# The first block of a convolution and SiLU kernel: up matmuls on 128 rows without ordering reads, exponents clamped on GpSimd, splits on VectorE

## The chip, the cores and the metric

One Trainium2 chip; the kernel runs on one of its cores. The time is that of one execution on the device in microseconds, the median of several runs. The profile comes from one execution of its own.

## The reference

A lightweight convolution feeds a two-layer SiLU network, all in float32:

```
w   = softmax(weight)                    # 8 heads x 7 taps
y   = causal conv of x (8, 4096, 192) along the sequence, one filter for each group of 24 channels
h   = y.reshape(32768, 192) @ w_in       # w_in  192 x 2048, float64 in memory
out = (h * sigmoid(h)) @ w_out           # w_out 2048 x 192, float64 in memory
```

The two weight matrices arrive as 64-bit floats, and the kernel makes 32-bit floats of them with integer instructions on their two halves.

## The kernel before

The 32768 tokens are done in 32 blocks of 1024 (`TT`), each of two halves of 512 (`TB`). The 192 channels are three pieces of 64: pieces 0 and 1 stand on partitions 0 to 63 and 64 to 127 of one set of tiles (`nats[0]`, `xts[0]`, `xs[0]`), piece 2 of both halves on those of another (`nats[1]`, `xts[1]`, `xs[1]`). A value that goes into the up matmuls is split into a high part, a low part and a mixed one (`split` for x, `Unit` for the weights), in a type that TensorE takes in one pass.

`PLAN` is a written order of tokens that each block follows from the second on: loads, transposes, taps (`conv`), splits, up matmuls (`A`, `B` with `w_a`, `C`, `E` with `w_b`), a scaling of the sums in PSUM on ScalarE (`X`), SiLU (`S`), sums and down matmuls. Within a block a pair of up matmuls works on two halves of the array's rows, and the two write different banks. Before a bank is written from the other half of the rows, VectorE reads one column of it into `dot` (`T`, `U`): the next matmul on the bank waits for that read.

The first block goes its own way, as the weights must be made ready beside it. All instructions of an engine stay in the order in which the code issues them (`pin`), and each engine works through its own list; SP's list holds nearly all DMA issues. In order:

- x and w_in are asked for on SP and ACT. `load_in(j, part, queue)` brings a quarter `j` of w_in: part 0 is rows 0 to 127 (one DMA), part 1 rows 128 to 191 (two DMAs).
- The taps are made on TensorE from the softmax. Two sets of diagonal matrices (`diag_of`) let TensorE do the first block's convolution (`conv_on_pe`) in three pieces of 512 columns.
- Twelve `Unit`s convert the weights: for each quarter of w_in one of part 0 (512 words a partition, to `w_a`) and one of part 1 (256 words, to `w_b`), then four quarters of w_out (768 words, to `wd`). A unit takes the exponent bits (`exponent`), the sign of the low byte and the clamped exponent (`on_act`: a Sign and two Relus on ScalarE), the mantissa and a sticky bit, and puts the number together (`rounded`). A unit of w_in is then split: `high`, `scaled` on ScalarE, `lower`, `between` on VectorE, and for part 1 `spread` copies half of `w_b` to the other 64 partitions by two DMAs on the GpSimd queue. `work(u)` runs unit u together with the split of unit u - 1.
- `woven` interleaves those steps with the sixteen up tiles (`of_up`: quarter j, chunk c, two banks each) in the order of the code. In tile i's turn stand A and B of that tile and C, T, E, U, X, S of the one before.
- `load_out(q, queue)` asks for a quarter of w_out with two DMAs; the third and fourth reuse buffers that earlier units must have read.
- After the sixteenth tile come the down matmuls of the first block (`down_plain`, 96 on `g` and `wd`), the transposes, the stores, and on VectorE `combine_out`, which changes `wd` for the later blocks. The second block's loads, taps and splits (`first_`) run beside the down matmuls.

Nearly all instructions are issued through a wrapper, so the profile gives them line 142; matmuls of the blocks have line 457. They are told apart by their tiles: `g` (weights being converted, and SiLU's results), `ps` (the banks), `w_a`, `w_b`, `wd`, `xs`, `dot`.

Of the kernel before, what the change touches and what calls it, by code (L numbers as in the profile page):

```python
# [8 lines left out]
F32 = mybir.dt.float32  # L9
# [3 lines left out]
AF = mybir.ActivationFunctionType  # L13
ALU = mybir.AluOpType
# [4 lines left out]
def kernel(  # L19
# [17 lines left out]
    B, S, D = x.shape  # L37
    H, K = weight.shape
    NT = B * S
    DFF = moe_w_in.shape[1]  # L40
    P = 128
# [4 lines left out]
    TB = 512  # L46
# [3 lines left out]
    NJ = NCH // 4  # L50
    SQ = 32
    HT = TB // 2
    SPLIT = 4096.0
# [140 lines left out]
    def g_slot(j, c, n):  # L194
        return g_all[:, j // 2, 2 * c + n, j % 2, :]
# [25 lines left out]
    for sign, base in ((1, 0), (-1, grp - 1)):  # L221
# [18 lines left out]
        base=0,  # L240
# [25 lines left out]
    def load_in(j, part, queue):  # L266
        t = raw(("i", j))
        if part == 0:
            to = t[:, 0 : 2 * CA].rearrange("p (a e c) -> p a e c", a=2, e=2)
            queue.dma_start(out=to, in_=in_a[:, :, 2 * j : 2 * j + 2, :])  # L270
        else:
            to = t[:, 2 * CA : 2 * WC].rearrange("p (e c) -> p e c", e=2)
            for a in range(2):
                queue.dma_start(out=rows(to, a), in_=in_b[:, a, 2 * j : 2 * j + 2, :])

    def load_out(q, queue):
        t = raw(("o", q)).rearrange("p (a e d) -> p a e d", a=2, e=2)
        for a in range(2):
            queue.dma_start(out=t[:, a, :, :], in_=out32[a, q])
# [1 line left out]
    scratch = flat(g_all[:, 0, 8:11])  # L281
    low_all = flat(g_all[:, 1, 8])
    ONE = 1 << 20
    edges = const.tile([P, 2], F32, name="edges")
    vec.memset(edges[:, 0:1], float(1151 * ONE))
    vec.memset(edges[:, 1:2], float(255 * 8 * ONE))
    BELOW = 1.0 - 2.0**-13

    class Unit:
# [25 lines left out]

        def exponent(self):
            vec.tensor_single_scalar(self.ex, self.hi, 0x7FF * ONE, op=ALU.bitwise_and)

        def on_act(self):
            act.activation(self.st, self.byte, AF.Sign)  # L320
            act.activation(self.ex, self.ex, AF.Relu, bias=edges[:, 0:1], scale=-1.0)
            act.activation(self.ex, self.ex, AF.Relu, bias=edges[:, 1:2], scale=-8.0)

        def mantissa(self):
            vec.tensor_scalar(
# [17 lines left out]
                out=self.w, in0=m, scalar=2.0**-44, in1=self.ex.bitcast(F32), op0=ALU.mult, op1=ALU.mult  # L343
            )

        def high(self):
            act.activation(self.to[0], self.w, AF.Copy, scale=BELOW)

        def lower(self):
            vec.tensor_tensor(self.low, self.w, f32(self.to[0]), op=ALU.subtract)  # L350

        def scaled(self):
            act.activation(self.to[1], self.low, AF.Copy, scale=SPLIT)

# [23 lines left out]
    def heat(times):  # L378
        for _ in range(times):
# [35 lines left out]
    def turn_in(b, k):  # L415
        vec.transpose(xts[k][:, pad:], flat(nats[k]))
# [38 lines left out]

    def mm(to, lhs, rhs, start=False):
        return pin(nc.tensor.matmul(to, lhs, rhs, start=start, stop=True, skip_group_check=True))  # L457
# [140 lines left out]
    did.update((0, t) for t in base if t[0] in "QD" or t.split(".")[0] in (*SUMS, *PREP, "st"))  # L598

    units = [Unit(2 * j + part, ("i", j), part) for j in range(NJ) for part in range(2)]  # L600
    units += [Unit(q, ("o", q), None) for q in range(NJ)]

    def begin(u):
        if u < len(units):
            units[u].exponent()
            units[u].on_act()

    def work(u):

        now, was = (units[i] if 0 <= i < len(units) else None for i in (u, u - 1))  # L610
        split_ = was is not None and was.part is not None
        if split_:
            was.high()
        if now:
            now.mantissa()
        yield
        if split_:
            was.lower()
        if now:
            now.sticky()  # L620
        if split_:
            was.scaled()
        yield
        if split_:
            was.between()
            was.spread()
        yield
        if now:
            now.rounded()
            begin(u + 1)  # L630
            if now.key == ("o", 0):
                load_out(3, sync)
# [10 lines left out]
    diags = [flat(g_all[:, 0, s_])[:, 0 : K * P].rearrange("p (i c) -> p i c", c=P) for s_ in (6, 7)]  # L643

    def diag_of(k):
        for i in range(K):
            act.activation(diags[k][:, i, :], one_hot, AF.Copy, scale=taps[:, k, i : i + 1])

    def conv_on_pe(to, k, first):
        for i in range(K):  # L650
            mm(to, diags[k][:, i, :], xts[k][:, first + i : first + i + TB], start=i == 0)

    def drain(stream):
        for _ in stream:
            pass

    turn_in(0, 0)
    begin(0)
    diag_of(0)
    conv_on_pe(banks[0], 0, 0)  # L660
    turn_in(0, 1)
    halo_in(0, 2)
    drain(work(0))
    diag_of(1)
    conv_on_pe(banks[1], 0, TB)
    conv_on_pe(banks[2], 1, 0)
    split(0, 0, "h", banks[0], ts(0, TB))
    next_ = work(1)
    next(next_)
    split(0, 0, "l", banks[0], ts(0, TB))  # L670
    next(next_)
    split(0, 0, "d", banks[0], ts(0, TB))
    next(next_)
    drain(next_)
    split(0, 0, "h", banks[1], ts(1, TB))
    next_ = work(2)
    next(next_)
    split(0, 0, "l", banks[1], ts(1, TB))
    next(next_)
    split(0, 0, "d", banks[1], ts(1, TB))  # L680
    split(0, 1, "h", banks[2])
    next(next_)
    split(0, 1, "l", banks[2])
    split(0, 1, "d", banks[2])
    drain(next_)
    for _ in range(3):
        homes.append(homes.pop(0))

    def of_up(i):

        now = "%d%d" % divmod(i, 4) if i < 4 * NJ else ""
        was = "%d%d" % divmod(i - 1, 4) if i else ""
        for t in (["A.%s0", "C.%s", "T.%s"], ["B.%s0", "E.%s", "U.%s"], ["A.%s1", "X.%s0", "X.%s1"], ["B.%s1", "S.%s0", "S.%s1"]):
            who = now if t[0][0] == "A" else was
            if who:
                yield lambda t=t, who=who: [step(0, x_ % who) for x_ in t]

    def of_work(u):
        stream = work(u)
        for _ in range(4):  # L700
            yield lambda stream=stream: next(stream, None)
# [69 lines left out]
```

## Time and profile before

| what | us |
|---|---|
| median of 3 runs | 2286.57 (2285.32 to 2289.86) |
| profiled execution, its own time | 2284.52 |
| its span | 2282.8 |
| PE busy | 2238.4 (98%) |
| DVE busy | 1816.4 (80%) |
| ACT busy | 1323.4 (58%) |
| POOL busy | 14.8 (1%) |

PE is TensorE's matmuls, PEld its weight loads, DVE VectorE, ACT ScalarE, POOL GpSimd, SP the engine that issues DMAs. Times of rows count from the span's start. A row of an order in time reads: start, length, engine, line, operation, output <- input, shapes, count, and in brackets the idle time before it and what ended it. A row of waits reads: who waited for whom, us in total, times, longest. A row of groups reads: count | busy us, mean ns of one | idle time before and what ended it. Rows of one engine that follow each other can overlap a little, so one row's start to the next's is what an instruction takes in a full engine.

### The profile page before, as it was taken

Reading aid. Unit: us, or ns where it says so; the run is one execution under the profiler, and the core shown is the slowest. Engines: PE = TensorE matmul, PEld = TensorE weight load, DVE = VectorE, ACT = ScalarE, POOL = GpSimd, SP = SyncE. Lnnn points to the kernel's source line nnn. Section 1 sums busy time; section 2 is a strip of 40 time slices with the busy share of each in tenths; the row PEclk is TensorE's granted clock in tenths of the full one; section 3 lists DMA queues with packets and bytes.
Section 4 is the critical chain, followed back from the end, with each engine's and each line's share of the span. In section 5 each row is a group of like instructions: output and inputs, shape, how many; then the busy total and the mean of one; then the engine's idle time right before and its main releaser. Section 6 shows DMA issues by size and latency. Waiting matters only on the chain.

```text
span 2282.8 us, 47340 instructions
## 1 busy us (share of the span) xinstructions
PE 2238.4 (98%) x19386; PEld 1679.2 (74%) x19386; DVE 1816.4 (80%) x3049; ACT 1323.4 (58%) x2708; POOL 14.8 (1%) x58
## 2 busy tenths in 40 slices
PE   7789999999999999999999999999999999999998
PEld 4447777777777777777777777777777777777775
DVE  4658877888877888877888877888877888877866
ACT  5735666555666555666555566555566555566543
POOL 0000000000000000000000000000000000000000
PEclk8899999999999999999999999999999999999999
DMA  4210111011111011111011111011111011111001
GB/s 104 63 28 15 29 29 20 10 29 29 29 29 21 9 29 29 29 29 25 5 29 29 29 29 26 6 26 29 29 29 29 6 24 29 29 29 29 8 8 29
DMA packets 406122, 61.25 MB, mean 27 GB/s; under 512 B 401936, under 2 KB 403984, under 8 KB 405904
## 3 DMA queue, kind: packets, MB, share of 16 engines
q1 hardware_dynamic: 400176, 56.00, 14.4%
q8 instruction: 151, 2.47, 0.5%
q0 software_dynamic: 512, 1.57, 0.3%
q10 hardware_dynamic: 5216, 0.66, 0.2%
q14 instruction: 67, 0.55, 0.1%
HBM read 31.46 MB, written 25.17 MB: 25 GB/s over the span
## 4 chain that ended last, share of the span: by engine, by line
PE 97%; ACT 1%; DMA 1%; DVE 1%; SPq 0%; issue 0%; DVEq 0%; ACTq 0%
PE ps L457 97%; ACT g L142 1%; ACT ps L142 0%; DMA w_b<-w_b 0%; SPq L142 0%; DMA g<-in_moe_w_in_dram 0%; DVE g L142 0%; DVE wd L142 0%; DVE fin L142 0%; ACT w_b L142 0%; DVE xs L142 0%; ACT L142 0%; ACT wd L142 0%; DVE dot L142 0%; DVE w_a L142 0%
## 5 line engine op out<-in xcount | busy, mean ns | idle before, releaser
L457 PE MATMUL ps<-g,wd 128*64 128x256 f32 (+1 forms) x10112 | 1127.2, 384 | 0.0
L457 PEld LDWEIGHTS ps<-g,wd 128*64 128x64 f32 x10112 | 720.5, 137 | 396.9 <-issue 36.0
L142 DVE TENSOR_TENSOR g<-g 128x1024 f32<-128x1024 f32 x806 | 951.2, 1218 | 9.2 <-PE ps L457 5.6
L457 PE MATMUL ps<-xs,w_a 64*128 64x512 f32 x6144 | 899.6, 393 | 22.2 <-DVE dot L142 15.5
L142 ACT ACTIVATE ps<-ps 128x512 f32<-128x512 f32 (+1 forms) x1117 | 585.1, 581 | 313.7 <-PE ps L457 265.9
L457 PEld LDWEIGHTS ps<-xs,w_a 64*128 64x128 f32 x6144 | 639.2, 185 | 124.2 <-DVE dot L142 34.2
L142 ACT ACTIVATE g<-ps 128x512 f32<-128x512 f32 x1024 | 561.3, 616 | 50.2 <-PE ps L457 41.8
L457 PE MATMUL ps<-xs,w_b 64*128 64x512 f32 x3072 | 537.2, 394 | 7.2 <-DMA w_b<-w_b 7.2
L142 DVE COPY dot<-ps 128x1 f32<-128x1 f32 x1024 | 160.6, 157 | 382.1 <-PE ps L457 372.2
L457 PEld LDWEIGHTS ps<-xs,w_b 64*128 64x128 f32 x3072 | 330.5, 186 | 54.8 <-issue 11.5
L142 DVE SCALAR_TENSOR_TENSOR nat<-xt,taps,nat 128x1024 f32<-128x1024 f32 (+1 forms) x372 | 368.8, 1005 | 1.8 <-ACT nat L142 1.4
L142 ACT COPY fin<-ps 128x256 f32<-128x256 f32 (+1 forms) x127 | 47.8, 376 | 424.1 <-PE ps L457 424.1
L142 DVE TENSOR_TENSOR fin<-fin,ps 128x256 f32<-128x256 f32 x248 | 95.6, 404 | 19.2 <-PE ps L457 19.2
L142 DVE STREAM_TRANSPOSE fin<-fin 128x256 f32<-128x256 f32 (+1 forms) x189 | 83.0, 440 | 17.2 <-ACT fin L142 15.9
L142 ACT ACTIVATE nat<-xt,taps 128x1024 f32<-128x1024 f32 (+1 forms) x62 | 57.9, 936 | 16.3 <-DVE xt L142 14.5
L142 DVE STREAM_TRANSPOSE xt<-nat 128x512 f32<-128x512 f32 (+1 forms) x64 | 61.5, 963 | 3.5 <-ACT xt L142 2.5
L142 DVE SCALAR_TENSOR_TENSOR xs<-xs 128x512 fp32r<-128x512 f32 x65 | 60.9, 937 | 0.2
L142 DVE TENSOR_TENSOR xs<-nat,xs 128x1024 fp32r<-128x1024 f32 (+1 forms) x62 | 59.0, 952 | 0.0
L142 ACT ACTIVATE xs<-nat 128x1024 fp32r<-128x1024 f32 (+1 forms) x62 | 52.5, 846 | 10.9 <-DVE nat L142 10.9
L142 ACT ACTIVATE fin<-ps 128x256 f32<-128x256 f32 x93 | 35.8, 385 | 39.6 <-PE ps L457 39.6
L142 ACT COPY xt<-xt 64x6 f32<-64x6 f32 x56 | 10.9, 195 | 52.9 <-DVE xt L142 52.3
L142 ACT COPY ps<-zeros 128x256 f32<-128x256 f32 x62 | 23.6, 381 | 1.0
(58 smaller groups left out, 204.7 us busy)
## 6 DMA issues: line engine op xcount, KB each, us to landing
out_dram<-fin SPq DMA_DIRECT2D x244, 96.0 KB, 2.5
nat<-in_x_dram SPq DMA_DIRECT2D x126, 128.0 KB, 3.0
nat<-in_x_dram SPq DMA_DIRECT2D x128, 64.0 KB, 2.4
g<-in_moe_w_out_dram SPq DMA_DIRECT2D x4, 384.0 KB, 7.3
w_b<-w_b POOLq DMA_DIRECT2D x8, 192.0 KB, 3.0
fin<-in_moe_w_out_dram SPq DMA_DIRECT2D x4, 384.0 KB, 4.8
g<-in_moe_w_in_dram SPq DMA_DIRECT2D x2, 512.0 KB, 5.2
fin<-in_moe_w_in_dram SPq DMA_DIRECT2D x2, 512.0 KB, 6.8
```

Source lines behind the costliest of these rows:

```text
L142: return lambda *args, **kw: pin(getattr(self.engine, name)(*args, **kw))
L457: return pin(nc.tensor.matmul(to, lhs, rhs, start=start, stop=True, skip_group_check=True))
```

## The change

Only the first block's code changes, and the conversion of the weights.

- Up matmuls of the first block: `A` and `B` use all 128 rows, both pieces of channels in one matmul, one bank after the other; `C` and `E` keep 64 rows each, one bank each. `T` and `U` are gone. The order by tiles is A of tile i, then B, E and S of tile i - 2, then C and X of tile i; A of the first three tiles stands ahead of the loop.
- A unit's clamped exponent is made by two GpSimd instructions in place of ScalarE's two Relus; the Sign stays on ScalarE. `high` goes to VectorE, so a unit's split is three VectorE instructions and one of ScalarE, and it comes in the unit's own `work`. The next unit's exponent stands at the beginning of `work`.
- Part 1 of each quarter of w_in (with `spread`) is loaded and converted ahead of part 0, and `spread` is issued on SP's queue.
- The convolution of the third piece is done by ScalarE and VectorE (`conv(0, 1, i)`) in place of TensorE; the diagonal matrices are made once, and stand ahead of the first unit. A SiLU on one column, with its table load, stands behind the exponential of the softmax.

```diff
@@ Unit
         def exponent(self):
             vec.tensor_single_scalar(self.ex, self.hi, 0x7FF * ONE, op=ALU.bitwise_and)
-
-        def on_act(self):
             act.activation(self.st, self.byte, AF.Sign)
-            act.activation(self.ex, self.ex, AF.Relu, bias=edges[:, 0:1], scale=-1.0)
-            act.activation(self.ex, self.ex, AF.Relu, bias=edges[:, 1:2], scale=-8.0)
+            pool.tensor_scalar(
+                self.ex, self.ex, scalar1=float(896 * ONE), scalar2=float(1151 * ONE), op0=ALU.max, op1=ALU.min
+            )
+            pool.tensor_scalar(
+                self.ex, self.ex, scalar1=float(896 * ONE), scalar2=8.0, op0=ALU.subtract, op1=ALU.mult
+            )
...
-        def high(self):
-            act.activation(self.to[0], self.w, AF.Copy, scale=BELOW)
-
-        def lower(self):
+        def split(self):
+            vec.tensor_scalar(self.to[0], self.w, scalar1=BELOW, scalar2=None, op0=ALU.mult)
             vec.tensor_tensor(self.low, self.w, f32(self.to[0]), op=ALU.subtract)
-
-        def scaled(self):
             act.activation(self.to[1], self.low, AF.Copy, scale=SPLIT)
-
-        def between(self):
             vec.scalar_tensor_tensor(
...
         def spread(self):
             if self.part:
                 for a in range(2):
-                    pool.dma_start(
+                    sync.dma_start(
...
+    load_in(0, 1, sync)
     load_in(0, 0, sync)
...
+    act.activation(warm, warm, AF.Silu)
     for i in range(4, 8):
         load(0, i, sync)
-    load_in(0, 1, sync)
     for j in (1, 2, 3):
-        for part in range(2):
+        for part in (1, 0):
             load_in(j, part, sync)
...
-    units = [Unit(2 * j + part, ("i", j), part) for j in range(NJ) for part in range(2)]
+    units = [Unit(2 * j + i, ("i", j), 1 - i) for j in range(NJ) for i in range(2)]
...
+        now = units[u]
+        begin(u + 1)
+        now.mantissa()
+        now.sticky()
         yield
+        now.rounded()
+        if now.key == ("o", 0):
+            load_out(3, sync)
         yield
+        if now.part is not None:
+            now.split()
+            now.spread()
         yield
...
+    def up_first(what, i):
+        j, c = divmod(i, 4)
+        if what == "A":
+            held[i] = [homes.pop(0) for _ in range(2)]
+        to = held[i]
+        if what in "AB":
+            for n in range(2):
+                for v in range(2) if what == "A" else (2,):
+                    mm(to[n], w_a[:, v, j, c, :], xs[0][:, v, ts(n, TB)], what == "A" and v == 0)
+        elif what in "CE":
+            for v in range(2) if what == "C" else (2,):
+                for n in range(2):
+                    mm(to[n], rows(w_b, n)[:, v, j, (c + 2 * n) % 4, :], rows(xs[1], n)[:, v, :])
...
+    AHEAD = 3
+
+    def tile_steps(i):
+        for what, k in (("A", i), ("B", i - 2), ("E", i - 2), ("S", i - 2), ("C", i), ("X", i)):
+            if 0 <= k < NT_ and not (what == "A" and i < AHEAD):
+                yield lambda what=what, k=k: up_first(what, k)
...
     turn_in(0, 0)
+    for n in range(2):
+        for i in range(K):
+            mm(banks[n], diag[:, i, :], xts[0][:, n * TB + i : n * TB + i + TB], i == 0)
...
+    turn_in(0, 1)
+    halo_in(0, 2)
+    conv(0, 1, 0)
+    drain(first_)
+    drain(work(1))
+    for what in "hld":
+        split_pe(0, what)
+    for i in range(1, 4):
+        conv(0, 1, i)
+    for what in "hld":
+        split_pe(1, what)
+    for i in range(4, K):
+        conv(0, 1, i)
+    for i in range(AHEAD):
+        up_first("A", i)
+    for what in "hld":
+        split(0, 1, what)
+    drain(work(2))
     load_out(0, sync)
     for j in range(NJ):
-        ups = [f for i in range(4 * j, 4 * j + 4 + (j == NJ - 1)) for f in of_up(i)]
-        woven(ups, [*of_work(2 * j + 3), *of_work(2 * j + 4)])
+        ups = [f for i in range(4 * j, 4 * j + 4 + (2 if j == NJ - 1 else 0)) for f in tile_steps(i)]
+        woven(ups, [f for u in (2 * j + 3, 2 * j + 4) for f in of_work(u)])
```

More of the change, by code (lines that the diff above doesn't have):

```diff
@@ L283 @@
     ONE = 1 << 20
-    edges = const.tile([P, 2], F32, name="edges")
-    vec.memset(edges[:, 0:1], float(1151 * ONE))
-    vec.memset(edges[:, 1:2], float(255 * 8 * ONE))
     BELOW = 1.0 - 2.0**-13
@@ L597 @@
     prep = [t for t in base if t.split(".")[0] in PREP]
-    did.update((0, t) for t in base if t[0] in "QD" or t.split(".")[0] in (*SUMS, *PREP, "st"))
-    units = [Unit(2 * j + part, ("i", j), part) for j in range(NJ) for part in range(2)]
+    did.update((0, t) for t in base if t[0] in "QDABCEXSTU" or t.split(".")[0] in (*SUMS, *PREP, "st"))
+    units = [Unit(2 * j + i, ("i", j), 1 - i) for j in range(NJ) for i in range(2)]
     units += [Unit(q, ("o", q), None) for q in range(NJ)]
@@ L605, in begin @@
             units[u].exponent()
-            units[u].on_act()
     def work(u):
[L610 to L615, printed above, removed]
-        yield
[L617 to L622, printed above, removed]
+        now = units[u]
+        begin(u + 1)
+        now.mantissa()
+        now.sticky()
+        yield
+        now.rounded()
+        if now.key == ("o", 0):
+            load_out(3, sync)
         yield
-        if split_:
-            was.between()
-            was.spread()
+        if now.part is not None:
+            now.split()
+            now.spread()
         yield
[L628 to L632, printed above, removed]
     def woven(*streams):
@@ L641, in woven @@
                     s_[k]()
[L643 to L651, printed above, removed]
+    diag = flat(g_all[:, 0, 7])[:, 0 : K * P].rearrange("p (i c) -> p i c", c=P)
     def drain(stream):
@@ L655, in drain, with of_work, split_pe @@
             pass
-    turn_in(0, 0)
+    def of_work(u):
+        stream = work(u)
+        for _ in range(3):
+            yield lambda: next(stream, None)
+    def split_pe(n, what):
+        split(0, 0, what, banks[n], ts(n, TB))
+    held = {}
+    def up_first(what, i):
[11 more added lines that the diff above has]
+                    mm(to[n], rows(w_b, n)[:, v, j, (c + 2 * n) % 4, :], rows(xs[1], n)[:, v, :])
+        elif what == "X":
+            for n in range(2):
+                act.activation(to[n], to[n], AF.Copy, scale=1.0 + 1.0 / SPLIT)
+        else:
+            for n in range(2):
+                act.activation(g_slot(j, c, n), to[n], AF.Silu)
+            homes.extend(held.pop(i))
@@ new lines @@
+    NT_ = 4 * NJ
+    AHEAD = 3
[4 more added lines that the diff above has]
+    for i in range(K):
+        act.activation(diag[:, i, :], one_hot, AF.Copy, scale=taps[:, 0, i : i + 1])
+    turn_in(0, 0)
+    for n in range(2):
+        for i in range(K):
+            mm(banks[n], diag[:, i, :], xts[0][:, n * TB + i : n * TB + i + TB], i == 0)
@@ L658 @@
+    homes.append(homes.pop(0))
+    homes.append(homes.pop(0))
     begin(0)
-    diag_of(0)
-    conv_on_pe(banks[0], 0, 0)
+    first_ = work(0)
+    next(first_)
     turn_in(0, 1)
     halo_in(0, 2)
[L663 to L701, printed above, removed]
+    conv(0, 1, 0)
[13 more added lines that the diff above has]
+        split(0, 1, what)
```

## The prediction

> **What bounds the kernel now.** I read the page, then the busy time by stretches of the first 200 us, the waits there, and the order in time on each engine. From the second block on PE is 9 tenths or more busy in nearly every slice of the page, and the change touches nothing there; so only the time at which the first block lets go can move. That block has three parts: a prologue to 30.3 us, the up matmuls with the conversion of the weights to 99.8, and the plain down matmuls to 142.8. The stretches (PE, PEld, DVE, ACT, POOL, granted clock, DMA):
>
> ```profile
> 30.30:99.80 69.50, 50.12 (x291) 32.38 (x290) 36.89 (x96) 53.88 (x100) 4.67 (x7) 0.88 0.27 67
> 99.80:142.80 43.00, 43.00 (x196) 13.85 (x196) 24.95 (x29) 8.77 (x14) 1.24 (x1) 0.96 0.00 1
> ```
>
> In the middle part no engine is full: ACT has 53.9 of 69.5 us, PE 50.1, DVE 36.9. In the last part PE is full. Who waits for whom in the middle part, the reads that make the order, and the first down matmul:
>
> ```profile
> DVE dot L142 <- PE ps L457: 24.0, 20, 2.8
> PE ps L457 <- DMA w_b<-w_b: 7.2, 3, 2.5
> PE ps L457 <- DVE dot L142: 5.5, 4, 2.5
> L142 DVE COPY dot<-ps 128x1 f32<-128x1 f32 x32 | 5.0, 157 | 24.2 <-PE ps L457 24.0
> 99.76 1.12 PE L457 MATMUL ps<-g,wd 128*64 128x512 f32 x2
> ```
>
> The 32 reads of one column hold DVE for 24 us until PE has come by; the conversion of the weights queued behind them comes late, ACT's share of it too, and PE waits for the copied half of w_in (7.2 us) and for the reads (5.5). Down matmuls start at 99.76. That is the mark: each microsecond by which they start earlier is one of the span, as long as PE stays full to their end.
>
> **Prices.** From one row's start to the next's, on ACT and on DVE:
>
> ```profile
> 60.83 1.06 ACT L142 ACTIVATE ps<-ps 128x512 f32<-128x512 f32 x2
> 61.81 1.07 ACT L142 ACTIVATE g<-ps 128x512 f32<-128x512 f32 x2
> 62.77 0.42 ACT L142 ACTIVATE w_b<-g 128x256 fp32r<-128x256 f32 x1
> ...
> 72.61 0.95 ACT L142 ACTIVATE wd<-g 128x768 int32<-128x768 uint8 x1
> 73.40 1.95 ACT L142 ACTIVATE g<-g,edges 128x768 int32<-128x768 int32 x2
> ```
>
> ```profile
> 56.78 0.42 DVE L142 SCALAR_TENSOR_TENSOR g<-g,fin 128x256 f32<-128x256 int32 x1
> ...
> 57.91 0.42 DVE L142 TENSOR_SCALAR g<-fin 128x512 int32<-128x512 int32 x1
> 58.24 0.43 DVE L142 COPY dot<-ps 128x1 f32<-128x1 f32 x2
> ...
> 63.11 0.69 DVE L142 SCALAR_TENSOR_TENSOR g<-g,fin 128x512 f32<-128x512 int32 x1
> ...
> 65.04 0.29 DVE L142 TENSOR_SCALAR g<-fin 128x256 int32<-128x256 int32 x1
> ...
> 77.86 1.82 DVE L142 SCALAR_TENSOR_TENSOR g<-g 128x768 f32<-128x768 int32 x2
> ...
> 80.63 0.55 DVE L142 TENSOR_SCALAR g<-fin 128x768 int32<-128x768 int32 x1
> ```
>
> ACT: a pair of X 0.98, a pair of S 0.96, a scaled half 0.4 (256 wide, so some 0.6 for 512), a Sign 0.79 (768, so some 0.53 and 0.26). DVE: the three two-input instructions of `rounded` 1.93 (512), 2.77 (768), 1.13 (256), so 0.64, 0.92 and 0.38 for one; a one-input instruction 0.33 (512), by proportion some 0.47 and 0.2. A w_a unit with the whole new split on DVE (three of one input: exponent, mantissa, high; six of two: sticky, rounded, low, between) is then 3 x 0.33 + 6 x 0.64 = 4.8, a w_b unit 2.9, an out unit (no split) 4.6. High has no DVE row: between a one-input row and a two-input one, 0.33 and 0.64, I take the first, as it has one input (the other end adds 2 us over the path).
>
> **The change, part by part.** Gone are the 32 reads with what waits behind them, and ACT's Relus and highs. ACT's share from the first X on is 16 x 1.94 for X and S and 7 for eight Signs (4.7) and five scaled halves (2.6): 38 us. PE makes as many passes: three 128-row matmuls for each bank in place of three 64-row pairs. The copy of w_b, a whole unit ahead of its use and issued by SP, lies beside the w_a unit; if that cover went, the 7.2 us above would come back. The Silu table load goes into ACT's idle time before 7.5. The conv of the third piece goes from PE to DVE. With its waits gone, DVE is the path until unit 8 (w_out's first quarter) is rounded. The rows for its beginning:
>
> ```profile
> 5.55 4.42 SPq L142 DMA_DIRECT2D g<-in_moe_w_in_dram  x5
> 8.82 0.71 DVE L142 STREAM_TRANSPOSE xt<-nat 128x512 f32<-128x512 f32 x1 [0.83 <-DMA nat<-in_x_dram]
> L142 DVE SCALAR_TENSOR_TENSOR nat<-xt,taps,nat 128x512 f32<-128x512 f32 x6 | 4.5, 751 | 0.2
> ```
>
> Two more issues stand on SP ahead of the second x tile, 0.88 each, so its transpose ends at 9.5 + 1.8 = 11.3. Behind it DVE has the rest of unit 0 (2.1), unit 1 (4.7), six splits of x (6 x 0.64 = 3.8), six taps (4.5), two waits for ACT's high of x (1.2, by ACT's rows of 0.6) and unit 2 with the next exponent (3.0): 19.3, so 30.6. Units 3 to 7 are 3 x 4.8 + 2 x 2.9 = 20.2, and unit 8 with unit 9's exponent 4.6: 55.4, without GpSimd.
>
> GpSimd now runs two instructions for each unit. On this path are those of units 2 to 9: 16, over 2 x 3840 = 7680 columns. The trace has none like them. What it has of POOL:
>
> ```profile
> 0.81 0.30 POOL L142 MEMSET sel<- 8x256 f32 x1 [0.29 <-POOLq L755]
> 2.20 0.28 POOL L142 TENSOR_SCALAR_AFFINE_SELECT g<-g 128x128 f32<-128x128 f32 x1
> 2.43 0.13 POOL L142 MEMSET xt<- 128x6 f32 x2
> 79.71 1.02 POOL L142 COPY xt<-xt 128x6 f32<-128x6 f32 x1
> 79.72 0.99 DVE L142 SCALAR_TENSOR_TENSOR wd<-g 128x768 f32<-128x768 f32 x1
> 180.59 0.19 POOL L142 COPY xt<-xt 128x6 f32<-128x6 f32 x1 [63.09 <-DVE dot L142]
> ```
>
> With 0.1 us fixed (the small memsets), 256 columns written cost 0.8 ns each and 128 selected ones 1.4 ns. I take 1.4, since the select also reads and computes; 0.8 is the lower end and twice the select, 2.8, the upper. The copy of six columns took 1.02 us beside a two-input DVE instruction of 0.99, against 0.19 elsewhere: POOL stood still meanwhile. If it is so the other way too, all of GpSimd's time adds to DVE's: 16 x 0.1 + 7680 x 1.4 ns = 12.4, and unit 8 is rounded at 67.8. The Trainium skill (SBUF — State Buffer, Who interferes with whom) says that a VectorE instruction with two SBUF inputs and a GpSimd one that reads SBUF exclude each other for an instruction's whole length; the copy agrees for the one direction, no row shows the other. The Trainium skill (GPSIMD Engine Reference, Performance versus the Vector engine) speaks against this change: elementwise work is about twice as slow there, 2.2 ns per column with two inputs; by that price the time would be 2276.
>
> Then w_out. Its last two quarters are asked for on SP behind unit 8:
>
> ```profile
> 79.75 0.90 SPq L142 DMA_DIRECT2D g<-in_moe_w_out_dram  x2
> 80.70 1.15 SPq L142 DMA_DIRECT2D fin<-in_moe_w_out_dram  x2
> fin<-in_moe_w_out_dram SPq DMA_DIRECT2D x2, 384.0 KB, 6.2
> fin<-in_moe_w_out_dram SPq DMA_DIRECT2D x4, 384.0 KB, 4.8
> ```
>
> Before, no wait of that part was for w_out: DVE came to unit 10 late enough. Now it comes there at once, and ACT's Sign of unit 10 stands ahead of X of the 13th tile: a new wait, with X and S of the last four tiles queued behind it on ACT and PE waiting for those. The last of the four issues starts 1.5 after unit 8, at 69.3, and lands 6.2 later, at 75.5. Then ACT has that Sign, four X, five S and the last Sign: 0.8 + 3.9 + 4.8 + 0.8 = 10.3; down matmuls start one S (1.0) before the end: 84.8.
>
> **The sum.** 99.8 - 84.8 = 15.0 earlier. What DVE has after unit 8, three units of 4.6 and at most the 25 us of the second stretch above, ends by 67.8 + 8 of wait + 39 = 115, before PE is through at 84.8 + 43 = 127.8, so it is late for nobody. The profiled execution took 2284.5 (span 2282.8): 2284.5 - 15.0 = 2269.5. The median of the three runs, 2286.6, lies 2 us above it; that stays inside the range. About 0.2%, 4.6 us, is what a measurement of this kernel tells from no change.
>
> **Rivals.** (1) No exclusion: GpSimd works beside DVE for nothing. ACT reaches the scaled half of unit 6 after 8 X, 6 S and four Signs and three scaled halves (1.6 each), at 30.6 + 16.8 = 47.4; behind it on SP are the w_b copies and the second quarter of w_out (2), landing 4.8 later: 54.2. Unit 8 takes its 4.6 from there: 58.8 in place of 67.8, so 2260.5. For it: no row shows DVE held by POOL. Were the loads no wait either, ACT alone would give 30.6 + 38 - 1 = 67.6, or 2252, the floor.
>
> (2) Slower than before: GpSimd's integer arithmetic is slow, on DVE's path from unit 2 to unit 9. At 2.8 ns it adds 7680 x 1.4 = 10.8: 2280. The gain is used up at 1.4 + 15.0 / 7.68 = 3.35 ns; at 4.5 ns the time is 2293. For it: no row prices such an instruction; against it: both POOL rows with work in them are at or under 1.4 ns.
>
> (3) The 128-row weight load isn't hidden and each such matmul costs double:
>
> ```profile
> L457 PEld LDWEIGHTS ps<-xt,g 128*128 128x128 f32 x42 | 8.6, 209 | 15.2 <-issue 13.0 <-ACT g L142 2.0 <-ACT xs L142 0.2
> 167.76 1.57 PE L457 MATMUL ps<-xs,w_a 64*128 64x512 f32 x12
> ```
>
> Six pairs in 1.4 us are 0.23 a pair, so a tile would need 6 x 0.23 = 1.4 more on PE, 3.4 in all. Up to the wait at 75.5 that is hidden; the last four tiles take 13.6 in place of 9.3: 2274. Against it: a 128-row load takes no longer than its row's 0.21.
>
> **How the numbers follow.** The forecast, with its neighbours in price (2262 to 2275), 0.56; rival 1 0.13; rival 2 0.25, of which 0.10 still faster by over 0.2%, 0.06 within it, 0.09 slower; rival 3 0.06. So faster 0.85, same 0.06, slower 0.09. The range runs from 2256, half way from rival 1 to the floor, to 2284, where the upper price with 1 us for high and 2 us for the median ends.
>
> **What would show it.** No dot reads before 100 us, and down matmuls starting at 80 to 90. GpSimd's 512-wide rows, start to start, at 0.6 to 1.0 us, and DVE idle beside them. An idle time on ACT and DVE before unit 10, ended by the w_out transfer, of several us. No wait of PE for the copy of w_b. I am wrong in the main point if unit 8 is rounded after 80, or if PE has idle time before 125 that DVE's preparation ends.

## The result, and the profile after

The changed kernel takes 2267.73 us (median of four runs, 2266.66 to 2267.96) against 2285.95 for the kernel before (2285.03 to 2289.86): ratio 0.9916, interval 0.9899 to 0.9933. The forecast was 2269.5, faster. The profiled execution took 2267.96 with a span of 2266.2, that is 16.6 less span than before.

The stretches of the first block after the change (columns as before: busy time and instructions of PE, PEld, DVE, ACT, POOL, then granted clock, DMA share, GB/s):

```profile
33.70:66.60 32.90, 31.82 (x140) 19.05 (x140) 31.33 (x52) 28.72 (x58) 24.92 (x13) 0.91 0.32 89
66.60:74.50 7.90, 1.20 (x6) 0.67 (x4) 1.38 (x3) 1.42 (x3) 1.54 (x2) 0.75 0.99 246
74.50:84.00 9.50, 9.37 (x30) 5.04 (x30) 9.36 (x9) 8.23 (x16) 9.26 (x4) 0.67 0.20 31
84.00:125.40 41.40, 41.40 (x196) 13.75 (x194) 24.07 (x27) 6.15 (x11) 4.11 (x3) 1.00 0.00 0
```

The middle part of before, 69.5 us in which nothing was full, has become 32.9 us in which PE and DVE are both nearly full, then 7.9 us in which no engine has more than 1.6 us of work and the DMA engines are 0.99 busy, then 9.5 us at a granted clock of 0.67. The standstill is the forecast wait for w_out. In the waits from 30 to 84 us, in the order in time on ACT, DVE and SP, and on PE:

```profile
ACT wd L142 <- DMA fin<-in_moe_w_out_dram: 7.3, 1, 7.3
DVE g L142 <- DMA fin<-in_moe_w_out_dram: 7.2, 2, 6.9
PE ps L451 <- ACT ps L142: 11.4, 3, 6.7
```

```profile
64.78 1.46 DVE L142 SCALAR_TENSOR_TENSOR wd<-g 128x768 f32<-128x768 f32 x1
64.81 0.88 SPq L142 DMA_DIRECT2D g<-in_moe_w_out_dram  x2
65.74 0.98 SPq L142 DMA_DIRECT2D fin<-in_moe_w_out_dram  x2
73.08 0.91 ACT L142 ACTIVATE wd<-fin 128x768 int32<-128x768 uint8 x1 [7.34 <-DMA fin<-in_moe_w_out_dram]
74.53 1.27 PE L451 MATMUL ps<-xs,w_a 128*128 128x512 f32 x2 [6.72 <-ACT ps L142]
83.97 41.42 PE L451 MATMUL ps<-g,wd 128*64 128x512 f32 x192
```

Unit 8 is rounded at 66.24 (64.78 + 1.46). The quarter that unit 10 needs, `fin`, is asked for behind the fourth one, `g`, which had to wait on SP for unit 8; the wait for it ends at 73.08. Sixteen X and S later the down matmuls start, at 83.97 in place of 99.76. No `dot` read is left ahead of 100 us, and PE has no wait for the copy of `w_b`.

### The profile page after: what moved, and what is told of

Read it like the earlier page. It is cut to its first block, busy times and chain, and to the rows that moved or that the text cites. A ratio compares the mean times of both kernels' runs of the same rounds, so it can differ in the third digit from the quotient of the medians.

```text
span 2266.2 us, 47061 instructions
## 1 busy us (share of the span) xinstructions
PE 2229.3 (98%) x19276; PEld 1671.2 (74%) x19276; DVE 1831.4 (81%) x3029; ACT 1302.0 (57%) x2671; POOL 59.5 (3%) x74
## 4 chain that ended last, share of the span: by engine, by line
PE 96%; DVE 2%; DMA 1%; SPq 0%; ACT 0%; issue 0%; DVEq 0%; ACTq 0%
PE ps L451 96%; DVE g L142 1%; SPq L142 0%; DMA fin<-in_moe_w_out_dram 0%; DMA g<-in_moe_w_in_dram 0%; DVE nat L142 0%; DVE fin L142 0%; DVE xs L142 0%; ACT g L142 0%; DVE wd L142 0%; ACT ps L142 0%; DVE w_a L142 0%; DVE w_b L142 0%; ACT xs L142 0%; ACT wd L142 0%
## 5 line engine op out<-in xcount | busy, mean ns | idle before, releaser
L451 PE MATMUL ps<-xs,w_a 64*128 64x512 f32 (+1 forms) x6048 | 890.0, 392 | 24.6 <-ACT ps L142 11.4
L451 PEld LDWEIGHTS ps<-xs,w_a 64*128 64x128 f32 (+1 forms) x6048 | 633.4, 185 | 126.6 <-ACT ps L142 28.1
L451 PE MATMUL ps<-xs,w_b 64*128 64x512 f32 x3072 | 529.0, 395 | 1.5 <-ACT xs L142 1.3
L142 DVE SCALAR_TENSOR_TENSOR nat<-xt,taps,nat 128x512 f32<-128x512 f32 (+1 forms) x378 | 373.2, 1001 | 1.9 <-ACT nat L142 1.4
L451 PEld LDWEIGHTS ps<-xs,w_b 64*128 64x128 f32 x3072 | 324.2, 185 | 53.5 <-issue 17.3
L142 ACT ACTIVATE nat<-xt,taps 128x512 f32<-128x512 f32 (+1 forms) x63 | 58.7, 933 | 16.3 <-DVE xt L142 14.7
L142 ACT ACTIVATE xs<-nat 128x512 fp32r<-128x512 f32 (+1 forms) x63 | 53.1, 843 | 17.2 <-DVE nat L142 17.2
L142 DVE TENSOR_TENSOR xs<-nat,xs 128x512 fp32r<-128x512 f32 (+1 forms) x63 | 59.7, 948 | 0.7 <-ACT xs L142 0.7
L142 POOL TENSOR_SCALAR g<-g 128x256 int32<-128x256 int32 (+2 forms) x24 | 50.6, 2108 | 33.5 <-DVE g L142 32.5
L142 POOL COPY xt<-xt 128x6 f32<-128x6 f32 x24 | 5.6, 235 | 1507.6 <-DVE dot L142 1426.4
```

The source lines that it names most:

```text
L142: return lambda *args, **kw: pin(getattr(self.engine, name)(*args, **kw))
```

## The experiments

Four theories run through the expectations. A: VectorE's list of conversions sets when unit 8 is rounded, and behind it the load of w_out sets the tail. B: GpSimd holds VectorE only near the beginning of its instructions, while it reads, some 6 us in all. C: GpSimd holds VectorE for the whole length of its instructions. D: PE's 2.48 us for a tile, from the first X on, sets the end.

They started from these rows of the kernel after. GpSimd's clamps, in the order in time of POOL (two instructions to a row):

```profile
34.25 2.71 POOL L142 TENSOR_SCALAR g<-g 128x256 int32<-128x256 int32 x2 [0.23 <-DVE g L142]
39.88 3.95 POOL L142 TENSOR_SCALAR g<-g 128x512 int32<-128x512 int32 x2 [2.92 <-DVE g L142]
54.13 6.18 POOL L142 TENSOR_SCALAR g<-g 128x768 int32<-128x768 int32 x2 [0.49 <-DVE g L142]
```

One takes 1.3, 1.9 or 3.1 us (256, 512, 768 columns): 4 to 5 ns a column, about three times the forecast price of 1.4. PE's tiles, in its order in time:

```profile
45.77 1.65 PE L451 MATMUL ps<-xs,w_a 128*128 128x512 f32 x6
47.35 0.96 PE L451 MATMUL ps<-xs,w_b 64*128 64x512 f32 x6
48.25 1.65 PE L451 MATMUL ps<-xs,w_a 128*128 128x512 f32 x6
```

From 45.77 to 48.25 is one tile, 2.48 us: 1.58 for the six 128-row matmuls and 0.90 for the three pairs.

The kernel before ran beside each of these on the same chip, at 2285.1 to 2285.2. All diffs but one are against the kernel after or an experiment named there.

### The third quarter of w_out asked for earlier

```diff
         now.rounded()
+        if now.key == ("i", 3) and now.part == 0:
+            load_out(2, sync)
         if now.key == ("o", 0):
             load_out(3, sync)
...
-        if j == 2:
-            load_out(2, sync)
```

> The changed kernel with the third quarter of w_out asked for as soon as unit 7 has been rounded, ahead of the fourth, instead of behind it and behind unit 8. Theory A (the forecast's path: VectorE up to unit 8, then this transfer, then the last four tiles): the wait of ScalarE and VectorE before unit 10 (7.3 and 6.9 us) goes nearly all, the half-speed clock behind it too, down matmuls start at 76 to 78 instead of 84.0, time 2260 to 2262. Rival (the wait only moves): the fourth quarter, still behind unit 8 and beside the loads of x, lands as late as the third did, and ScalarE waits at unit 11 instead; start at 80 to 82, time 2264 to 2266.

Measured: 2259.64 (2258.12 to 2260.75), ratio 0.9889 [0.9875, 0.9902]. What is left of the wait for w_out is 0.65 us, ahead of unit 9, and the down matmuls start earlier but take longer (waits, PE's order in time, and two stretches):

```profile
DVE g L142 <- DMA fin<-in_moe_w_out_dram: 0.7, 1, 0.7
74.61 43.12 PE L451 MATMUL ps<-g,wd 128*64 128x512 f32 x192
74.60:77.60 3.00, 3.00 (x10) 0.92 (x10) 2.97 (x3) 1.38 (x4) 2.92 (x2) 0.57 0.00 0
77.60:80.60 3.00, 3.00 (x14) 0.96 (x12) 2.93 (x5) 0.00 (x0) 2.94 (x2) 0.86 0.00 0
```

So the standstill was worth 9.4 us at the start of the down part (83.97 to 74.61) and hung on one line: the quarter needed first was queued behind the one that had to wait. Of the 9.4, 1.7 is lost again, as the granted clock is 0.57 and 0.86 at the beginning of the down part, which takes 43.1 in place of 41.4.

### The clamps on VectorE

```diff
-            pool.tensor_scalar(
+            vec.tensor_scalar(
...
-            pool.tensor_scalar(
+            vec.tensor_scalar(
```

> The changed kernel with the two clamp instructions of each unit on VectorE instead of GpSimd. Theory B (GpSimd holds VectorE only while it reads its input, some 0.8 ns a column at its start, 6 us in units 2 to 9): VectorE loses those holds and gains 16 one-input instructions, also some 6 us; unit 8 is rounded at 65 to 68 as before, time 2266 to 2269. Theory C (the forecast's: GpSimd holds VectorE for its whole length, 31.5 us of rows in units 2 to 9): VectorE has some 25 us less, unit 8 is rounded as early as ScalarE and TensorE let it, at 56 to 60, time 2260 to 2263.

Measured: 2268.46 (2267.35 to 2268.71), ratio 0.9928 [0.9914, 0.9941], no different from the kernel after. VectorE, now with two more instructions for each unit, reaches the end of unit 8 and the wait as before:

```profile
65.84 0.96 DVE L142 SCALAR_TENSOR_TENSOR wd<-g 128x768 f32<-128x768 f32 x1
73.33 0.92 ACT L142 ACTIVATE wd<-fin 128x768 int32<-128x768 uint8 x1 [7.34 <-DMA fin<-in_moe_w_out_dram]
83.75 41.42 PE L451 MATMUL ps<-g,wd 128*64 128x512 f32 x192
```

Unit 8 is rounded at 66.80 (65.84 + 0.96) against 66.24. GpSimd's clamps cost VectorE about as much as VectorE would need to do them itself, as theory B has it. Were VectorE held for their whole length, 29.8 us in the seven rows of POOL from 30.08 to 67.40, taking them away would have shown; C is out.

### The first clamp twice

```diff
             pool.tensor_scalar(
                 self.ex, self.ex, scalar1=float(896 * ONE), scalar2=float(1151 * ONE), op0=ALU.max, op1=ALU.min
             )
+            pool.tensor_scalar(
+                self.ex, self.ex, scalar1=float(896 * ONE), scalar2=float(1151 * ONE), op0=ALU.max, op1=ALU.min
+            )
```

> The changed kernel with the first clamp instruction of each unit issued twice on GpSimd (the second time it changes nothing), 36 instead of 24 instructions there. Theory B (a hold only while GpSimd reads): eight more holds in units 2 to 9, 3 us, and some more since GpSimd itself becomes full; unit 8 at 69 to 72, time 2270 to 2274. Theory C (held for the whole length): 16 us more on VectorE, unit 8 at 82, time 2283 or more.

Measured: 2272.73 (2270.89 to 2273.46), ratio 0.9945 [0.9932, 0.9957]. On VectorE at unit 8:

```profile
69.30 0.96 DVE L142 SCALAR_TENSOR_TENSOR g<-g 128x768 int32<-128x768 int32 x1 [2.68 <-POOL g L142]
70.29 1.46 DVE L142 SCALAR_TENSOR_TENSOR wd<-g 128x768 f32<-128x768 f32 x1
```

Unit 8 is rounded at 71.75, 5.5 later, though GpSimd has some 15 us more to do there (half of those 29.8). About half of the 5.5, 2.68, is a new thing: GpSimd works without a gap from 31.5 to 78.6, and at unit 8 its result is late. With two instructions a unit VectorE never waited for it from 30 to 84 us; with three GpSimd is full, and VectorE waits at unit 8. What is left, 2.8 (1.4 of it ahead of unit 2), is near the 3 that B gave for eight more holds, and far from C's 16.

### No clamp at all

```diff
-            pool.tensor_scalar(
...
-            pool.tensor_scalar(
...
```

> The changed kernel without the two clamp instructions of each unit on any engine (the exponents stay unclamped, so the weights are not the reference's). Theory B (GpSimd holds VectorE while it reads, 6 us in units 2 to 9, and nothing else hangs on it): VectorE's longer rows (0.86, 0.88, 1.31, 1.58, 1.46 us) go back to 0.42, 0.69, 0.95, unit 8 is rounded at 59 to 61 in place of 66.2, and the w_out transfer lands at 67 to 68; ScalarE comes to unit 10's Sign at about 65 all the same, so its wait falls from 7.3 to 2 to 3 us, down matmuls start at 78 to 80, time 2262 to 2264. Rival D (TensorE's 2.48 us a tile sets the stage up to 66 us, and unit 8 with it through ScalarE): unit 8 stays at 64 or later, time 2266 or more.

Measured: 2263.17 (2262.49 to 2264.84), ratio 0.9904 [0.9891, 0.9918]. It leaves out the clamps, so it shows VectorE's list without GpSimd. Its rows of units 7 and 8, with ScalarE's scaled half of unit 6 ahead of them; then VectorE's in the kernel after:

```profile
50.02 0.48 ACT L142 ACTIVATE w_b<-g 128x256 fp32r<-128x256 f32 x1
49.24 0.69 DVE L142 SCALAR_TENSOR_TENSOR fin<-fin,g 128x512 int32<-128x512 int32 x1
52.02 0.43 DVE L142 TENSOR_SCALAR w_a<-g 128x512 fp32r<-128x512 f32 x1
57.19 0.56 DVE L142 TENSOR_SCALAR g<-fin 128x768 int32<-128x768 int32 x1 [3.29 <-DMA fin<-in_moe_w_out_dram]
60.98 0.96 DVE L142 SCALAR_TENSOR_TENSOR wd<-g 128x768 f32<-128x768 f32 x1
69.12 0.91 ACT L142 ACTIVATE wd<-fin 128x768 int32<-128x768 uint8 x1 [7.08 <-DMA fin<-in_moe_w_out_dram]
```

```profile
54.30 1.31 DVE L142 SCALAR_TENSOR_TENSOR fin<-fin,g 128x512 int32<-128x512 int32 x1
57.70 0.93 DVE L142 TENSOR_SCALAR w_a<-g 128x512 fp32r<-128x512 f32 x1
60.36 0.56 DVE L142 TENSOR_SCALAR g<-fin 128x768 int32<-128x768 int32 x1 [0.29 <-DMA fin<-in_moe_w_out_dram]
```

An instruction that falls on the beginning of a 768-wide clamp is longer by 0.50 to 0.62 us, and the two-input ones behind it, still beside the 3.1 us clamp, have their usual length. B isn't the whole of it: the one-input row at 53.30, which lies across the end of the 512-wide clamps at 53.63, takes 0.75, and without clamps 0.55. Without clamps VectorE is through with unit 7 at 53.9 and with them at 60.07: 6.2 less (0.4 of it because w_in landed earlier in that run), as B has it. But then it waits 3.29 for w_out's second quarter, so unit 8 gains 4.3 and the time 4.6. That quarter was asked for at 51.81, on SP behind the copies of `w_b`, which had to wait for ScalarE's scaled half of unit 6 (50.02, where VectorE had its input ready at 48.06). This is the path that rival 1 described, and it hangs on PE's tiles in so far as ScalarE goes by them. In the kernel after, the same wait is 0.29 long: the two paths are nearly level there. The expected short wait ahead of unit 10 was wrong (7.1): ScalarE came there earlier too. D had said that unit 8 would stay at 64 or later; it is rounded at 61.94, with PE still at 2.48 a tile. So D alone doesn't set the end of the kernel after, but it stands close behind VectorE's list.

### The reads and 64-row matmuls of before, in the kernel after

```diff
+    def of_up(i):
+        ...
-    for i in range(AHEAD):
-        up_first("A", i)
...
-        ups = [f for i in range(4 * j, 4 * j + 4 + (2 if j == NJ - 1 else 0)) for f in tile_steps(i)]
+        ups = [f for i in range(4 * j, 4 * j + 4 + (j == NJ - 1)) for f in of_up(i)]
```

> The changed kernel with the up matmuls of the kernel before: 64 rows each, in pairs, with the ordering reads on VectorE, one tile behind; everything else as changed. If the reads were what held the first block (the forecast's first step), VectorE again waits some 15 to 25 us for TensorE, and down matmuls start at 95 to 102: 2279 to 2286. If the other parts of the change (splits and clamps off ScalarE, copied half first) are what brought it, the start stays at 84 to 88: 2268 to 2272.

Measured: 2279.28 (2277.81 to 2281.43), ratio 0.9976 [0.9967, 0.9984]; the down matmuls start at 95.93. The time is as expected, the way isn't. The waits from 30 to 96 us:

```profile
PE ps L451 <- DVE dot L142: 20.7, 10, 8.2
DVE g L142 <- DMA fin<-in_moe_w_out_dram: 8.0, 1, 8.0
DVE dot L142 <- PE ps L451: 7.4, 11, 3.0
```

VectorE waits only 7.4 us in its reads, where 15 to 25 were expected; PE waits 20.7 for them. VectorE's list is so full now that a read comes late, and when VectorE stands before unit 10 for w_out, the reads stand behind it (8.0 and 8.2). A read that orders another engine costs on the side that is ahead.

### Only the 128-row matmuls, in the kernel before

```diff
+    def up_first(what, i):
+        ...
+    for i in range(AHEAD):
+        up_first("A", i)
...
-        ups = [f for i in range(4 * j, 4 * j + 4 + (j == NJ - 1)) for f in of_up(i)]
+        ups = [f for i in range(4 * j, 4 * j + 4 + (2 if j == NJ - 1 else 0)) for f in tile_steps(i)]
```

> The kernel before with the up matmuls of the changed one alone (128-row tiles, no ordering reads, B, E and S two tiles behind); clamps and high stay on ScalarE, splits one unit late, copied half second and on GpSimd's queue, conv of the third piece on TensorE. If the reads were the main brake (24 us of VectorE's waits), ScalarE becomes the bound of the middle part with its 54 us of work: from 34 to about 88, less the last S; down matmuls start at 86 to 90, time 2271 to 2275. If it is the whole change together that counts and ScalarE's share or the late copy of w_b (three waits of 2.5 us) still brakes, the start stays at 93 to 97, time 2279 to 2283.

Measured: 2276.42 (2274.88 to 2276.95), ratio 0.996 [0.9947, 0.9972]; down matmuls at 92.04, between the two expectations. The waits from 30 to 96 us:

```profile
PE ps L457 <- DMA w_b<-w_b: 7.3, 3, 3.9
DVE g L142 <- ACT w_b L142: 12.7, 3, 5.3
DVE g L142 <- ACT w_a L142: 6.0, 3, 2.4
```

The new up matmuls alone are worth 8.7 us (2285.15 to 2276.42). That is the reads, the 128 rows and the new order of the tiles together; no run takes them apart, and only the waits point to the reads. Now VectorE waits for ScalarE's share of the split, 18.7, and PE for the late copy. The rest of the change alone, from the run ahead of this one, is worth 5.8 (2285.07 to 2279.28). Both together bring 17.4 (2285.1 to 2267.7), more than the 14.5 of the sum; by the start of the down matmuls it is 7.7 and 3.8 alone, and 15.8 together. Each part takes away a wait that the other runs into when it is alone.

### Part 0 first again

```diff
-    load_in(0, 1, sync)
     load_in(0, 0, sync)
+    load_in(0, 1, sync)
...
-        for part in (1, 0):
+        for part in (0, 1):
...
-    units = [Unit(2 * j + i, ("i", j), 1 - i) for j in range(NJ) for i in range(2)]
+    units = [Unit(2 * j + i, ("i", j), i) for j in range(NJ) for i in range(2)]
```

> The changed kernel with the copied part of each quarter of w_in loaded and converted second again, its copy still on SP's queue. If the order of the parts matters (the copy must lie beside the other part's unit), TensorE again waits for the copy at the first tiles of a quarter, 2 to 3 us each, time 2270 to 2276. If the split in the unit's own work is what brings the copy early enough, and the order is only a detail, TensorE waits for it at most once, time 2266 to 2269.

Measured: 2267.34 (2266.65 to 2267.83), ratio 0.9921 [0.9908, 0.9935]; down matmuls at 84.37, no wait of PE for the copy. The order of the two parts brings nothing here that a run can tell.

### The third piece's convolution back on TensorE

```diff
-    diag = flat(g_all[:, 0, 7])...
+    diag, diag1 = [flat(g_all[:, 0, s_])... for s_ in (7, 6)]
...
-    conv(0, 1, 0)
+    for i in range(K):
+        act.activation(diag1[:, i, :], one_hot, AF.Copy, scale=taps[:, 1, i : i + 1])
+    for i in range(K):
+        mm(banks[2], diag1[:, i, :], xts[1][:, i : i + TB], i == 0)
...
-    for what in "hld":
-        split(0, 1, what)
     drain(work(2))
+    for what in "hld":
+        split(0, 1, what, banks[2])
```

> The changed kernel with the convolution of the third piece on TensorE again (a second set of diagonal matrices), and unit 2 converted ahead of that piece's split. Theory A (VectorE's list sets the time of unit 8): its list is shorter by the six taps and a wait, 5 us; the first X comes at 28 to 30 in place of 33.7, unit 8 is rounded at 61 to 62 in place of 66.2, the w_out transfer lands 5 us earlier, down matmuls start at 78 to 80, time 2262 to 2264: this part of the change cost what it took from VectorE's beginning. Rival (TensorE's longer convolution takes its place, or its pace of 2.48 us a tile holds unit 8 through ScalarE): start at 82 to 84, time 2266 to 2268.

Measured: 2262.47 (2260.8 to 2262.79), ratio 0.9901 [0.9886, 0.9916]:

```profile
28.71 1.07 ACT L142 ACTIVATE ps<-ps 128x512 f32<-128x512 f32 x2 [1.31 <-PE ps L451]
59.85 1.47 DVE L142 SCALAR_TENSOR_TENSOR wd<-g 128x768 f32<-128x768 f32 x1
68.14 0.91 ACT L142 ACTIVATE wd<-fin 128x768 int32<-128x768 uint8 x1 [7.47 <-DMA fin<-in_moe_w_out_dram]
79.03 41.42 PE L451 MATMUL ps<-g,wd 128*64 128x512 f32 x192
```

With six taps off VectorE's list, unit 8 is rounded 4.9 earlier (61.32), the down matmuls start 4.9 earlier, and the wait is as long as ever. The first X comes 4.9 earlier too (28.71, in the kernel after 33.66), so the whole stage has moved: A and D both give this, and the run doesn't tell them apart. It gives the price: this part of the change, the six taps on VectorE with unit 2 behind the third piece's split, cost some 5 us.

### Unit 2 among the up tiles, on top of the earlier quarter

```diff
-    drain(work(2))
     load_out(0, sync)
...
-        woven(ups, [f for u in (2 * j + 3, 2 * j + 4) for f in of_work(u)])
+        woven(ups, [f for u in ((2, 3, 4) if j == 0 else (2 * j + 3, 2 * j + 4)) for f in of_work(u)])
```

> The changed kernel with the third quarter of w_out asked for behind unit 7, and with unit 2 converted beside the first up tiles instead of ahead of them (the first quarter of w_out is then asked for ahead of unit 2's copy). Theory D (TensorE paces the stage at 2.48 us a tile once the w_out wait is gone, so it has to begin earlier): the first X comes at 29 instead of 33.7, down matmuls start at 70 to 72 instead of 74.6, time 2255 to 2257. Rival A (VectorE's conversion paces it, TensorE waits for w_a of the next quarter): the stage begins earlier but TensorE waits before tiles 4, 8 or 12, start at 73 to 75, time 2258 to 2260.

Measured: 2257.84 (2257.58 to 2257.88), ratio 0.988 [0.9866, 0.9893], 1.8 under the run with the earlier quarter alone. In PE's order in time, and in the stretch at the beginning of the down part:

```profile
37.52 0.67 PE L451 MATMUL ps<-xs,w_a 128*128 128x512 f32 x1 [3.63 <-DVE w_a L142]
74.50 41.42 PE L451 MATMUL ps<-g,wd 128*64 128x512 f32 x192
74.50:77.50 3.00, 3.00 (x16) 1.05 (x16) 2.97 (x3) 1.37 (x4) 2.92 (x2) 1.00 0.01 1
```

PE begins its tiles earlier and then waits 3.63 for VectorE; the down matmuls start at 74.50, no earlier than 74.61. So D fails here: an earlier beginning of PE's tiles doesn't bring an earlier end, as VectorE's `w_a` isn't there yet. The 1.8 us lie in the down part: 41.4 in place of 43.1, at a clock of 1.00 from the beginning here and 0.57 there. The gain has another reason than the one it was made for.

### Both: the convolution on TensorE and the earlier quarter

> The same with the third quarter of w_out asked for behind unit 7. Theory A: with the shorter list on VectorE and no wait for w_out, the weights come 5 us earlier than in the run with that edit alone, and TensorE goes through its tiles at 2.48 us from about 29: down matmuls start at 69 to 71 instead of 74.6, time 2253 to 2256. Rival (the tiles are held by something else, ScalarE's list or the gaps of TensorE at the last tiles): start at 73 or later, time 2257 to 2259.

The edits are those of the two experiments. Measured: 2254.06 (2253.29 to 2254.29), ratio 0.9866 [0.9849, 0.9882]. This beats both kernels: 31 us under before, 13.7 under after.

```profile
33.00:66.00 33.00, 32.45 (x152) 19.42 (x154) 31.60 (x50) 31.19 (x62) 25.87 (x11) 1.00 0.37 105
70.34 41.42 PE L451 MATMUL ps<-g,wd 128*64 128x512 f32 x192
```

PE, DVE and ACT are all over nine tenths busy from 33 to 66, at full clock. The longest wait of one of the three for another there is 0.8. PE goes from most tiles to the next at its 2.48, so what theory D said of the kernel after is nearly so in this one: by these shares PE's tiles are as much the limit as VectorE's list.

### The clamps of w_in on ScalarE, on top of that

```diff
+            if self.part is not None:
+                act.activation(self.ex, self.ex, AF.Relu, bias=edges[:, 0:1], scale=-1.0)
+                act.activation(self.ex, self.ex, AF.Relu, bias=edges[:, 1:2], scale=-8.0)
+                return
```

> The same again with the clamped exponents of w_in's eight units on ScalarE (two Relus each), those of w_out on GpSimd. Theory B: VectorE loses the holds of units 2 to 7, about 4 us, but TensorE's 2.48 us a tile is then the pace and ScalarE has 9 us more in its list: no gain, 2253 to 2257. If VectorE is still the pace, 3 to 4 us less than the run without this edit: 2250 to 2252. If ScalarE's list becomes the bound: 2258 or more.

Measured: 2256.14 (2254.41 to 2257.44), ratio 0.9874 [0.9859, 0.9889]: no gain, and 2.1 more than without this edit. VectorE is held less, and gets to wait:

```profile
51.60 0.43 ACT L142 ACTIVATE w_b<-g 128x256 fp32r<-128x256 f32 x1
58.97 0.56 DVE L142 TENSOR_SCALAR g<-fin 128x768 int32<-128x768 int32 x1 [6.34 <-DMA fin<-in_moe_w_out_dram]
28.00:60.00 32.00, 29.39 (x135) 16.73 (x133) 23.85 (x49) 29.04 (x58) 6.19 (x3) 1.00 0.36 107
```

From 28 to 60 us VectorE is busy 23.9 and ScalarE 29.0, where it was 30.6 and 27.7 with all clamps on GpSimd; the down matmuls start at 73.21. ScalarE's list is late first: VectorE has the input of unit 6's scaled half ready at 45.24 (without this edit at 48.10), ScalarE comes to it at 51.60 (48.74), with no idle time ahead of it, and the two quarters of w_out stand on SP behind the copies that wait for it, until 53.35. So there is no gain, as expected, but it is ScalarE's list that holds the kernel, and not PE's 2.48 a tile.

## Why the prediction was right, and where it was wrong

The forecast, 15.0 us for the stated reason, was near: the mark moved by 15.8, and 16.6 came out of the span. Point by point:

| step | forecast | measured |
|---|---|---|
| second transpose of x done | 11.3 | 11.72 |
| unit 2 begins | 27.6 (30.6 less its 3.0) | 29.57 |
| units 2 to 8 on VectorE, without GpSimd | 27.8 | 30.6 (no clamp: 28.07 to 61.94, less the wait of 3.29) |
| GpSimd's time on that path | 12.4 (16 instructions, units 2 to 9) | 6 (29.57 to 66.24 in the kernel after, less those 30.6; the 14 instructions of units 3 to 9) |
| unit 8 rounded | 67.8 | 66.2 |
| w_out for unit 10 landed | 75.5 | 73.1 |
| from there to the down matmuls | 9.3 | 10.9 |
| down matmuls start | 84.8 | 83.97 |
| their length | 43.0 | 41.4 |

**The mechanism held.** The reads gone, VectorE the path until unit 8 (nearly: the work on unit 8 begins with a wait of 0.29 for w_out's second quarter, which hangs on ScalarE), w_out the new wait ahead of unit 10 with the last tiles behind it, no wait for the copy of `w_b`, and the second block's preparation in time. That the wait hangs on when the quarter is asked for was shown by asking sooner.

**Two terms were mis-sized, against each other.** The step "GpSimd's time adds to VectorE's, at 1.4 ns a column" was wrong twice. A clamp takes 1.3 us for 256 columns, 1.9 for 512, 3.1 for 768, which is 4 to 5 ns a column: above the 3.35 at which, by rival 2, the whole gain is used up. The kernel came out faster all the same because the other half of the step failed as well: VectorE isn't held for the whole length. The runs without clamps and with the clamps on VectorE put what it costs at about 6 us in units 2 to 8, a fifth of the clamps' 29.8. Neither the forecast nor rival 2 had that case. One of the forecast's signs failed in both halves with it: GpSimd's 512-wide rows were to stand 0.6 to 1.0 us apart, with VectorE idle beside them. Rival 1, no exclusion at all, gave 2260.5; the run without clamps, 2263.2, comes nearest to it, and there the path that rival 1 named did set unit 8, 3.1 later than it said (61.94 against 58.8).

The Trainium skill (SBUF — State Buffer, Who interferes with whom) gave the exclusion that the forecast carried over to this direction. Its rule that a two-input VectorE instruction contends with a GpSimd one that reads SBUF agrees with the lengthened rows (1.31 against 0.69). That the other side blocks for the whole instruction, which the section says in its line on the 2-port modes, does not agree: VectorE goes on beside a clamp of 3.1 us after some 0.6. That the hold is the clamp's reading is inferred from its growing with the columns (0.86 in place of 0.42 at a 512-wide one, 1.31 in place of 0.69 at a 768-wide one); no run isolates it. The Trainium skill (GPSIMD Engine Reference, Engine selection) calls one-input elementwise work on GpSimd "roughly line-rate"; here the 768-wide clamp took 3.1 us there, and VectorE's one-input row of that width is 0.56.

**VectorE's list was priced too short.** By 2.8 in units 2 to 8, as instructions that take the one before as input stand further apart than the prices had it (0.46 and 0.73 from start to start for 512 columns, against 0.33 and 0.64), and the whole began 2.0 later, 1.1 of it GpSimd's holds ahead of unit 2, where the sum had none (without clamps unit 2 begins at 28.07, 1.5 sooner, of which 0.4 is the earlier landing). These errors and the one in GpSimd's term have opposite signs: 27.6 + 27.8 + 12.4 = 67.8 was forecast, 29.6 + 30.6 + 6 = 66.2 came. So the nearness of the forecast time is in part luck.

**The clock was not in the sum.** Three stretches: the beginning of the down part before, and the second 3 us of PE's work behind its 10 us pause in the second block, before and after:

```profile
99.80:102.80 3.00, 3.00 (x10) 0.96 (x10) 2.96 (x6) 2.47 (x4) 0.00 (x0) 0.50 0.00 0
156.65:159.65 3.00, 3.00 (x22) 2.11 (x22) 2.14 (x5) 2.61 (x5) 0.00 (x0) 0.85 0.00 0
139.30:142.30 3.00, 3.00 (x16) 2.08 (x16) 2.15 (x5) 2.43 (x4) 0.00 (x0) 0.51 0.03 8
```

Before, the down part ran its first 3 us at half clock and took 43.0. After, the low clock lies behind PE's standstill, in the last tiles (0.67 in that stretch): the six 128-row matmuls at 77.31 take 2.9 in place of 1.65. The tail is 1.6 longer than forecast, the down part 1.6 shorter. With the standstill gone, in the run with the earlier quarter, the down part again began at 0.57. Of the 17.4 by which the down part ends earlier after the change, 0.7 is lost in the second block, where the clock comes back later.

**Rival 3** was half right: a tile takes PE 2.48, not the 2.0 of the forecast and not its 3.4. It cost little, as VectorE's list set the pace. Whether the changes between 128 and 64 rows, two in a tile, make the difference was not isolated.

## What to carry to other kernels

Look at which of two loads is needed first and which can be issued first before putting them on one queue: one line in the wrong place stood for 8 us here. When a wait goes, price the list of the engine behind it by rows that depend on each other, not by rows that stand beside each other. Moving work to an engine that stands idle isn't free where the two share something, but the price is what a run shows, neither nothing nor the whole length.

## What the runs showed that was not expected

An integer two-operation instruction on GpSimd took 4 to 5 ns a column, over five times VectorE's one-input instruction at 768 columns (3.1 against 0.56), yet held VectorE for only some 0.6 us at its beginning. The half clock at the beginning of a PE stretch isn't fixed: two kernels whose down matmuls start within 0.1 us of each other (74.61 and 74.50) differ by 1.7 us in that part, with 0.57 and 1.00 granted in its first 3 us. What decides it is open. And two parts of one change were worth 8.7 and 5.8 us alone, and 17.4 together.
